# Attention and two feed-forward blocks on one core: phi's row sums, its gate and the last block's scaling placed later, and an addition moved to VectorE

## The chip, the cores and the metric

The kernel runs on one core of a Trainium2 chip. The metric is the device time of one execution in microseconds (us). An execution is compared with others of the same kernel by the median of several runs.

## What is computed

Attention with a linear memory for 4 batches of 8 heads, 576 rows and 64 columns, and behind it two feed-forward blocks:

```python
scores = scale * np.matmul(q, k.transpose(0, 1, 3, 2))
scores = np.where(causal, -1000000000.0, scores)
scores = scores - scores.max(-1, keepdims=True)
a = np.exp(scores)
a /= a.sum(-1, keepdims=True) + 1e-09
local = np.matmul(a, v)
q_p = phi(q)                       # phi(x) = where(x > 0, x, exp(x) - 1) + 1
mem_ret = np.einsum('bhsd,bhde->bhse', q_p, M_prev)
mem_norm = np.einsum('bhsd,bhd->bhs', q_p, z_prev)[..., None] + 1e-06
mem_out = mem_ret / mem_norm
g = 1.0 / (1.0 + np.exp(-beta))[None, :, None, None]
out = g * mem_out + (1 - g) * local
# x: (2304, 512), the heads side by side
h = x @ w_in;  x = (h * np.tanh(softplus(h))) @ w_out      # 512 -> 2048 -> 512
out = (((x @ w1) * (x @ w2)) @ w3) @ w_out2                # 512 -> 1024 -> 512
```

## The kernel before, in words

The attention stage runs over 16 pairs of heads, `p` = 0 to 15, and one turn of the loop (L563) is called a period here. In a period the scores of pair `p` are made while the values of pair `p - 1` are multiplied and those of pair `p + 1` are prepared. The 576 rows of a head are cut into four blocks of 128 rows, numbered 0 to 3, and a last block that holds the remaining 64 rows of both heads.

For a block, `s_blocks` (L397) and `s_last` (L413) let TensorE write scores to a PSUM tile `psA`. VectorE adds the mask and takes the maxima (`maxed`, L389 and L390, a custom instruction and a read of its accumulator). ScalarE makes the exponentials and their sums (`expd`, L395). `normed` (L370) turns the sums to reciprocals (L376, L377) and scales the rows (L381): block by block on VectorE, and on GpSimd for the four numbers in `ON_POOL`. The scaled rows are transposed by TensorE and copied by ScalarE (`pt_g`, L438, copies at L447), and `pv` (L449) multiplies them by the values. The result is rounded by ScalarE (L468) and its remainder taken by VectorE (L79) into `xt`.

In a period the blocks come in the order 3, 2, then 0 and 1 together, then the last. `prep` makes transposed q and k of the next pair in between.

The memory part is `prep_phi` (L332). ScalarE takes the exponential of q (L340), GpSimd makes q + 1 (L341), VectorE joins both to phi (L342). GpSimd multiplies phi by z (L344, the tile `qz`), VectorE sums the rows (L351, the tile `dn`), GpSimd adds 1e-6 (L352), VectorE takes the reciprocal (L353) and multiplies by the gate (L354), and GpSimd multiplies phi by that (L357). `trans_phi` (L362) transposes the result one period later. `qz` and the tile of q + 1 share one buffer.

From pair 4 to pair 11 each period also decodes one piece of the first feed-forward weights, which lie in memory as 64-bit numbers: six VectorE steps (L110 to L121) and three GpSimd steps (L125, L76, L79). `drip` (L546) gives out a few of these steps at a time between the blocks. The tile `da` has one buffer, so the first step of a piece, L110, waits for the last GpSimd step of the piece before.

The order of the instructions comes from a scheduler, which keeps to the order edges written in the program: `tc.issue_after(i)` puts what stands in the block behind instruction `i` on `i`'s engine. `split_x[0]` is the last remainder that `pv` took, `taken[0]` the last maxima. Before, the row sums of phi and the last block's scaling carry the edge behind `split_x[0]`:

```python
            if split_x[0] is not None:
                k_.enter_context(tc.issue_after(split_x[0]))
            nc.vector.tensor_reduce(out=dn, in_=qz, axis=mybir.AxisListType.X, op=ALU.add)
        nc.gpsimd.tensor_scalar(out=dn, in0=dn, scalar1=1e-6, scalar2=1.0, op0=ALU.add, op1=ALU.mult)
```

Behind the attention stage come the two feed-forward blocks, which hold TensorE busy for most of the time.

Of the kernel before, what the change touches and what calls it, by code (L numbers as in the profile page):

```python
# [14 lines left out]
ALU = mybir.AluOpType  # L15
# [6 lines left out]
def fused_kernel(ctx: ExitStack, tc, q, k, v, M_prev, z_prev, beta, w_in, w_out, w1, w2, w3, w_out2, out):  # L22
    nc = tc.nc
    B, H, S, D = q.shape
# [3 lines left out]
    NP = H // 2  # L28
# [300 lines left out]
        st[p]["sum"] = ap_.tile([128, 9], F32, tag="sum", name="sum", bufs=2)  # L329
        st[p]["acc"] = ap_.tile([128, 10], F32, tag="acc", name="acc", bufs=2)  # L330

    def prep_phi(p):  # L332
        b, c = divmod(p, NP)
        qv = st[p]["q"]
        if c == 2 and b + 1 < B:
            load_m(b + 1)
        z = st[p]["z"]
        e = ep.tile([128, NB, 2, D], F32, tag="phie", name="phie", bufs=2)
        u = ep.tile([128, NB, 2, D], F32, tag="ptmp", name="phit", bufs=1)
        nc.scalar.activation(out=e, in_=qv, func=AF.Exp)  # L340
        nc.gpsimd.tensor_scalar(out=u, in0=qv, scalar1=1.0, scalar2=1.0, op0=ALU.add, op1=ALU.mult)  # L341
        nc.vector.scalar_tensor_tensor(out=e, in0=e, scalar=1.0, in1=u, op0=ALU.min, op1=ALU.max)  # L342
        qz = ep.tile([128, NB, 2, D], F32, tag="ptmp", name="qz", bufs=1)
        nc.gpsimd.tensor_tensor(  # L344
            out=qz, in0=e, in1=z[:, None, :, :].to_broadcast([128, NB, 2, D]), op=ALU.mult
        )
        dn = ep.tile([128, NB, 2], F32, tag="dn", name="dn", bufs=2)
        with ExitStack() as k_:
            if split_x[0] is not None:
                k_.enter_context(tc.issue_after(split_x[0]))  # L350
            nc.vector.tensor_reduce(out=dn, in_=qz, axis=mybir.AxisListType.X, op=ALU.add)  # L351
        nc.gpsimd.tensor_scalar(out=dn, in0=dn, scalar1=1e-6, scalar2=1.0, op0=ALU.add, op1=ALU.mult)  # L352
        nc.vector.reciprocal(out=dn, in_=dn)  # L353
        nc.vector.tensor_tensor(  # L354
            out=dn, in0=dn, in1=g_[:, 1:2, 2 * c:2 * c + 2].to_broadcast([128, NB, 2]), op=ALU.mult
        )
        nc.gpsimd.tensor_tensor(  # L357
            out=e, in0=e, in1=dn[:, :, :, None].to_broadcast([128, NB, 2, D]), op=ALU.mult
        )
        st[p]["e"] = e  # L360
# [9 lines left out]
    def normed(p, xs):  # L370

        d = st[p]
        og = ogp[:, p % NP]
        sl = slice(0, 8) if len(xs) > 1 else slice(8, 9)
        rv = d["sum"][:, sl]
        nc.vector.tensor_scalar(out=rv, in0=rv, scalar1=1e-9, scalar2=None, op0=ALU.add)  # L376
        nc.vector.reciprocal(out=rv, in_=rv)  # L377
        for ib, e in xs:
            s = s4[:, 0:S] if ib == 4 else d["s"][ib, e]
            x = 8 if ib == 4 else 2 * ib + e  # L380
            (nc.gpsimd if x in ON_POOL else nc.vector).tensor_scalar(  # L381
                out=s, in0=s, scalar1=d["sum"][:, x:x + 1], scalar2=og[:, x:x + 1], op0=ALU.mult, op1=ALU.mult
            )

    taken = [None]
    split_x = [None]
    copied = [None]

    def maxed(s, o, m, init, a):  # L389
# [59 lines left out]
    def pv(p):  # L449
        b, c = divmod(p, NP)  # L450
        d = st.pop(p)
        V, T, F = d["v"], d["t"], d["phi"]
        pm, pl = psX(), psF()[:, 0:64]
        M_ = mr[b % 2][:, c]
        hv = (UP, DN)
        mm(pm, M_.rearrange("p e d -> p (e d)"), F[:, 0:512], True, False)
        for jb in range(4):
            for e in range(2):
                t, x = T[jb, e, jb]
                mm(pm[hv[e], 128 * jb:512], V[:, jb, e], t[:, x:x + 512 - 128 * jb], False, jb == 3)  # L460
        for e in range(2):
            mm(pl[hv[e]], M_[:, e], F[:, 512:S], True, False)
        for jb in range(5):
            for e in range(2):
                mm(pl[hv[e]], V[:, jb, e], T[4, None, jb][:, hv[e]], False, jb == 4)
        for o, q0, q1 in ((pm, 0, 512), (pl, 512, S)):
            x = xl[b // 2][:, :, c, S * (b % 2) + q0:S * (b % 2) + q1]
            nc.scalar.copy(out=x[:, 0], in_=o[:, 0:q1 - q0])  # L468
            split_x[0] = sub(x[:, 1], o[:, 0:q1 - q0], x[:, 0]).ins

    gt = {}

# [90 lines left out]
    for p in range(NPAIR + 1):  # L563
# [15 lines left out]
        if now:  # L579
            in_turn(s_blocks, p, (3,))  # L580
            if decodes:
                drip(1)
        else:
            in_turn(next, h0)
        if old:
            in_turn(pt_g, p - 1, 1)
# [2 lines left out]
                in_turn(next, h0)  # L589
        if now:  # L590
            in_turn(s_blocks, p, (2,))
            if decodes:
                drip(1)
        if p == 0:
            gate_values(b_)
        if old:
# [25 lines left out]
            normed(p, [(i, e) for e in range(2) for i in range(4)])  # L622
        if p == 0:
            with tc.issue_after(taken[0]):
                prep_phi(0)
        if old:
            in_turn(pv, p - 1)
        if not now:
            split = split_y((0, 0), next(h0))
            early = {(0, 1): emit_h((0, 1))}  # L630
        if now:
            with ExitStack() as k_:
                if old:
                    k_.enter_context(tc.issue_after(split_x[0]))
                normed(p, [(4, None)])
            if decodes:
                drip(7)
        if new:
            with tc.issue_after(taken[0]):
                prep_phi(p + 1)  # L640
        if now and p > 0:
            in_turn(trans_phi, p)
    at.close()
# [248 lines left out]
```

## Time and profile before

| | us |
|---|---|
| median of 3 runs (1028.5 to 1029.44) | 1029.01 |
| the profiled execution | 1029.42 |
| its span, from the first to the last instruction | 1027.6 |

| engine | busy us | share of the span |
|---|---|---|
| TensorE (PE) | 974.8 | 95% |
| TensorE weight load (PEld) | 827.7 | 81% |
| VectorE (DVE) | 617.1 | 60% |
| ScalarE (ACT) | 501.4 | 49% |
| GpSimd (POOL) | 336.8 | 33% |

SP is SyncE, which issues most of the loads. The rows of a timeline give the start of an instruction in us from the start of the span, its length in us, the engine, the line, the operation, what it writes and reads with partitions x elements, and, in brackets, how long the engine had been idle and what ended that. A length can overlap the next instruction's by some 0.1 us, and several instructions of one line in a row are merged (x4).

### The profile page before, as it was taken

Reading aid. Unit: us, or ns where it says so; the run is one execution under the profiler, and the core shown is the slowest. Engines: PE = TensorE matmul, PEld = TensorE weight load, DVE = VectorE, ACT = ScalarE, POOL = GpSimd, SP = SyncE. Lnnn points to the kernel's source line nnn. Section 1 sums busy time; section 2 is a strip of 40 time slices with the busy share of each in tenths; the row PEclk is TensorE's granted clock in tenths of the full one; section 3 lists DMA queues with packets and bytes.
Section 4 is the critical chain, followed back from the end, with each engine's and each line's share of the span. In section 5 each row is a group of like instructions: output and inputs, shape, how many; then the busy total and the mean of one; then the engine's idle time right before and its main releaser. Section 6 shows DMA issues by size and latency. Waiting matters only on the chain.

```text
span 1027.6 us, 15098 instructions
## 1 busy us (share of the span) xinstructions
PE 974.8 (95%) x5584; PEld 827.7 (81%) x5584; DVE 617.1 (60%) x1364; ACT 501.4 (49%) x1016; POOL 336.8 (33%) x345
## 2 busy tenths in 40 slices
PE   6888888889999999999999999999989999999998
PEld 3555555556899999999999999988757888888897
DVE  5678889876366669885988476666973221121111
ACT  5777877776565655655555644442313221221212
POOL 5546686653143344545454212112550000000000
PEclk8999999999999999999999999999999999999999
DMA  7433443310131214232421662222410000100101
GB/s 158 116 70 95 109 109 93 69 30 17 46 123 48 96 62 164 65 112 87 148 103 63 246 228 80 77 78 85 165 48 1 20 22 1 42 1 1 41 1 62
DMA packets 93626, 81.73 MB, mean 80 GB/s; under 512 B 68720, under 2 KB 72816, under 8 KB 93552
## 3 DMA queue, kind: packets, MB, share of 16 engines
q1 hardware_dynamic: 92224, 80.44, 25.3%
q8 instruction: 44, 0.72, 0.3%
q10 hardware_dynamic: 1328, 0.33, 0.2%
q14 instruction: 30, 0.25, 0.1%
HBM read 65.54 MB, written 15.20 MB: 79 GB/s over the span
## 4 chain that ended last, share of the span: by engine, by line
PE 69%; DVE 15%; ACT 6%; DMA 3%; POOL 3%; issue 2%; SPq 1%; POOLq 0%; DVEq 0%; ACTq 0%
PE psA L63 37%; PE psX L63 15%; PE psF L63 14%; DVE s L390 2%; ACT s L395 2%; DVE draw L121 2%; DVE s L381 1%; PE psF L66 1%; ACT pt L447 1%; DVE da L117 1%; DMA draw<-in_moe_w_dram 1%; PE psX L66 1%; DVE phie L342 1%; DVE y L506 1%; DVE draw L120 1%
## 5 line engine op out<-in xcount | busy, mean ns | idle before, releaser
L63 PE MATMUL psA<-xt,wqt 128*128 128x384 f32 x1152 | 208.9, 337 | 2.4 <-DVE y L506 2.2
L125 POOL TENSOR_TENSOR da<-da,draw 128x512 f32<-128x512 f32 x72 | 100.8, 1408 | 326.3 <-DVE draw L121 282.1
L63 PEld LDWEIGHTS psA<-xt,wqt 128*128 128x128 f32 x1152 | 201.5, 189 | 3.9 <-DVE y L506 3.2
L63 PE MATMUL psX<-gh,wqt 128*128 128x384 f32 x480 | 122.3, 335 | 1.1 <-DVE x L673 1.1
L818 DVE TENSOR_TENSOR bs<-bs,psA 128x512 f32<-128x512 f32 (+1 forms) x40 | 25.4, 634 | 160.0 <-ACT bs L817 160.0
L63 PE MATMUL psA<-x2h,w12t 128*128 128x512 f32 (+1 forms) x384 | 107.1, 357 | 6.8 <-DVE bs L818 4.6
L817 ACT COPY bs<-psA 128x512 f32<-128x512 f32 (+1 forms) x40 | 21.8, 544 | 160.6 <-PE psA L63 150.6
L395 ACT ACTIVATE s<-s,acc 128x512 f32<-128x512 f32 (+2 forms) x144 | 85.5, 600 | 28.9 <-DVE acc L390 28.5
L66 PEld LDWEIGHTS psF<-ident,s 128*128 128x128 f32 x400 | 44.9, 145 | 55.8 <-ACT pt L447 26.8
L63 PE MATMUL psA<-x2s,w12t 128*128 128x512 f32 x384 | 89.7, 389 | 0.0
L66 PE MATMUL psF<-ident,s 128*128 128x128 f32 x400 | 66.4, 292 | 23.8 <-ACT pt L447 14.9
L63 PEld LDWEIGHTS psX<-gh,wqt 128*128 128x128 f32 x480 | 86.9, 188 | 2.2 <-DVE x L673 1.4
L493 ACT ACTIVATE y<-psA 128x384 f32<-128x384 f32 x96 | 41.9, 490 | 90.2 <-PE psA L63 90.1
L63 PEld LDWEIGHTS psA<-x2h,w12t 128*128 128x128 f32 x384 | 68.3, 189 | 20.8 <-DVE bs L818 5.0
L63 PEld LDWEIGHTS psA<-x2s,w12t 128*128 128x128 f32 x384 | 72.1, 188 | 14.9
L390 DVE CUSTOM_DVE_ANT_0 s<-psA,mask 128x512 f32<-128x512 f32 (+2 forms) x144 | 62.8, 480 | 31.0 <-PE psA L63 30.8
L506 DVE TENSOR_TENSOR y<-y,psA 128x384 f32<-128x384 f32 x96 | 48.6, 549 | 53.4 <-ACT y L504 53.4
L63 PE MATMUL psX<-gl,wqt 128*128 128x384 f32 x240 | 80.4, 336 | 0.0
L63 PE MATMUL psF<-gh,wqt 128*128 128x384 f32 x288 | 73.1, 334 | 0.0
L63 PE MATMUL psA<-room,w12t 128*128 128x512 f32 (+1 forms) x192 | 68.0, 354 | 0.0
L447 ACT COPY pt<-psF 128x512 f32<-128x512 f32 (+1 forms) x112 | 58.9, 540 | 17.7 <-PE psF L66 17.6
L63 PE MATMUL psX<-wft,room 128*128 128x512 f32 x216 | 61.6, 391 | 0.3 <-DVE wft L79 0.3
(117 smaller groups left out, 1871.7 us busy)
## 6 DMA issues: line engine op xcount, KB each, us to landing
draw<-in_moe_w_dram SPq DMA_DIRECT2D x32, 512.0 KB, 3.7
draw<-in_moe_w_out_dram SPq DMA_DIRECT2D x24, 512.0 KB, 3.5
draw<-in_moe_w_in_dram SPq DMA_DIRECT2D x16, 512.0 KB, 4.5
out_dram<-ob SPq DMA_DIRECT2D x18, 256.0 KB, 2.0
raw<-in_q_dram SPq DMA_DIRECT2D x32, 128.0 KB, 2.8
raw<-in_v_dram SPq DMA_DIRECT2D x32, 128.0 KB, 3.0
o_dram<-draw SPq DMA_DIRECT2D x8, 512.0 KB, 2.8
w_dram<-draw SPq DMA_DIRECT2D x8, 512.0 KB, 2.8
```

The source lines that it names most:

```text
L63: tail[0] = nc.tensor.matmul(o, lhsT=l, rhs=r, start=start, stop=stop).ins
L66: tail[0] = nc.tensor.transpose(o, src, ident).ins
L117: lambda: V.scalar_tensor_tensor(out=ai, in0=hw, scalar=-0x40000000, in1=ai, op0=ALU.bitwise_and, op1=ALU.bitwise_or),
L121: lambda: V.scalar_tensor_tensor(out=lw.bitcast(F32), in0=lw.bitcast(U32), scalar=2.0 ** -52, in1=hw.bitcast(F32), op0=ALU.mult, op1=ALU.mult,
L125: lambda: nc.gpsimd.tensor_tensor(out=a, in0=a, in1=lw.bitcast(F32), op=ALU.add),
L390: taken[0] = nc.vector.tensor_tensor_reduce(out=s, in0=o, in1=m, op0=ALU.add, op1=ALU.min, scale=-scale, scalar=init, accum_out=a,).ins
L395: nc.scalar.activation(out=s, in_=s, func=AF.Exp, scale=-1.0, bias=a, accum_out=r)
L447: copied[0] = nc.scalar.copy(out=t[:, 0:n], in_=o[:, 0:n]).ins
L493: nc.scalar.activation(out=y[m // 2][:, m % 2], in_=hp[m], func=AF.Tanh, scale=0.5)
L506: nc.vector.tensor_tensor(out=y[i][:, j], in0=y[i][:, j], in1=hp[2 * i + j], op=ALU.mult)
L817: nc.scalar.copy(out=bs, in_=pb)
L818: nc.vector.tensor_tensor(out=bs, in0=bs, in1=pa, op=ALU.mult)
```

## The change

`prep_phi` is cut in two. `phi_terms` makes phi and the product with z, and the product now stands behind GpSimd's scaling of the pair before (`scaled[0]`, set in `normed`). `phi_norm` makes the row sums, adds 1e-6 on VectorE, takes the reciprocal and multiplies by the gate. `phi_norm` of pair `p` and the last block's `normed` of pair `p - 1` move from the end of a period into the next one, behind the maxima of block 2, with an edge behind the last maxima taken. In the title of the change the blocks are counted from one, and block 2 is the third. One call of `drip` goes, so that the rest of the piece takes one step more.

```diff
-    def prep_phi(p):
+    def phi_terms(p):
...
-        nc.gpsimd.tensor_tensor(
-            out=qz, in0=e, in1=z[:, None, :, :].to_broadcast([128, NB, 2, D]), op=ALU.mult
-        )
+        with tc.issue_after(scaled[0]):
+            nc.gpsimd.tensor_tensor(
+                out=qz, in0=e, in1=z[:, None, :, :].to_broadcast([128, NB, 2, D]), op=ALU.mult
+            )
+        st[p]["e"] = e, qz
+
+    def phi_norm(p):
+        c = p % NP
+        e, qz = st[p]["e"]
         dn = ep.tile([128, NB, 2], F32, tag="dn", name="dn", bufs=2)
-        with ExitStack() as k_:
-            if split_x[0] is not None:
-                k_.enter_context(tc.issue_after(split_x[0]))
-            nc.vector.tensor_reduce(out=dn, in_=qz, axis=mybir.AxisListType.X, op=ALU.add)
-        nc.gpsimd.tensor_scalar(out=dn, in0=dn, scalar1=1e-6, scalar2=1.0, op0=ALU.add, op1=ALU.mult)
+        nc.vector.tensor_reduce(out=dn, in_=qz, axis=mybir.AxisListType.X, op=ALU.add)
+        nc.vector.tensor_scalar(out=dn, in0=dn, scalar1=1e-6, scalar2=None, op0=ALU.add)
         nc.vector.reciprocal(out=dn, in_=dn)
...
-            (nc.gpsimd if x in ON_POOL else nc.vector).tensor_scalar(
+            r = (nc.gpsimd if x in ON_POOL else nc.vector).tensor_scalar(
                 out=s, in0=s, scalar1=d["sum"][:, x:x + 1], scalar2=og[:, x:x + 1], op0=ALU.mult, op1=ALU.mult
             )
+            if x in ON_POOL:
+                scaled[0] = r.ins
...
         else:
+            normed(p - 1, [(4, None)])
             in_turn(next, h0)
...
             in_turn(s_blocks, p, (2,))
-            if decodes:
-                drip(1)
+            if old:
+                with tc.issue_after(taken[0]):
+                    normed(p - 1, [(4, None)])
+                    phi_norm(p)
...
         if p == 0:
             with tc.issue_after(taken[0]):
-                prep_phi(0)
+                phi_terms(0)
+                phi_norm(0)
...
-        if now:
-            with ExitStack() as k_:
-                if old:
-                    k_.enter_context(tc.issue_after(split_x[0]))
-                normed(p, [(4, None)])
-            if decodes:
-                drip(7)
         if new:
             with tc.issue_after(taken[0]):
-                prep_phi(p + 1)
+                phi_terms(p + 1)
+        if decodes:
+            drip(7)
```

The lines behind L332 move by a few numbers: the maxima are at L395, the scalings at L384, the row sums at L354, the addition at L355, reciprocal and gate at L356 and L357, the product with z at L345 and phi's last product at L360.

On VectorE, in a period that decodes, between the remainders of one pair and the first two blocks' maxima of the next, this order stood before (s_113 is the last block, s_1711 and s_1736 are blocks 3 and 2 of the first head, s_1783 is block 0, dn holds phi's row sums; of each block's maxima the first instruction is shown):

```order
L79 TENSOR_TENSOR xt_81<-psF,xt_81 128x64
L376 TENSOR_SCALAR sum<-sum 128x1
L351 TENSOR_REDUCE dn<-qz 128x10
L377 RECIPROCAL sum<-sum 128x1
L390 ISA s_1711,acc<-psA,mask 128x512
L381 TENSOR_SCALAR s_113<-s_113,sum,ogp 128x576
L353 RECIPROCAL dn<-dn 128x10
L354 TENSOR_TENSOR dn<-dn,gates 128x10
L390 ISA s_1736,acc<-psA,mask 128x384
L110 TENSOR_SCALAR da<-draw 128x512
L390 ISA s_1783,acc<-psA,mask 128x128
```

And this order stands there now (s_1702 and s_1727 are blocks 3 and 2, s_1782 is block 0):

```order
L79 TENSOR_TENSOR xt_81<-psF,xt_81 128x64
L395 ISA s_1702,acc<-psA,mask 128x512
L395 ISA s_1727,acc<-psA,mask 128x384
L379 TENSOR_SCALAR sum<-sum 128x1
L354 TENSOR_REDUCE dn<-qz 128x10
L380 RECIPROCAL sum<-sum 128x1
L110 TENSOR_SCALAR da<-draw 128x512
L355 TENSOR_SCALAR dn<-dn 128x10
L384 TENSOR_SCALAR s_113<-s_113,sum,ogp 128x576
L356 RECIPROCAL dn<-dn 128x10
L357 TENSOR_TENSOR dn<-dn,gates 128x10
L395 ISA s_1782,acc<-psA,mask 128x128
```

The sums, the gate and the last block's scaling have moved behind the maxima of blocks 3 and 2, and the addition has joined them.

On GpSimd, in the same period, from the product with z to q for the last block of the next pair (`qd`), this stood before (phit is q + 1, phie is phi, wqt the decoded weights):

```order
L344 TENSOR_TENSOR qz<-phie,zr 128x640
L381 TENSOR_SCALAR s_1783<-s_1783,sum,ogp 128x128
L381 TENSOR_SCALAR s_1711<-s_1711,sum,ogp 128x512
L125 TENSOR_TENSOR da<-da,draw 128x512
L352 TENSOR_SCALAR dn<-dn 128x10
L341 TENSOR_SCALAR phit<-raw 128x640
L76 TENSOR_SCALAR wqt<-da 128x512
L357 TENSOR_TENSOR phie<-phie,dn 128x640
L79 TENSOR_TENSOR wqt<-da,wqt 128x512
L324 TENSOR_TENSOR qd<-qt,own 128x128
```

And this stands there now (of the four scalings the first two are shown in both):

```order
L384 TENSOR_SCALAR s_1782<-s_1782,sum,ogp 128x128
L384 TENSOR_SCALAR s_1702<-s_1702,sum,ogp 128x512
L345 TENSOR_TENSOR qz<-phie,zr 128x640
L125 TENSOR_TENSOR da<-da,draw 128x512
L76 TENSOR_SCALAR wqt<-da 128x512
L79 TENSOR_TENSOR wqt<-da,wqt 128x512
L341 TENSOR_SCALAR phit<-raw 128x640
L360 TENSOR_TENSOR phie<-phie,dn 128x640
L324 TENSOR_TENSOR qd<-qt,own 128x128
```

The scalings have passed the product with z, the decoded piece has passed phi's two steps, and the addition is gone. TensorE's order is the same in both; on ScalarE one exponential of block 1 and a copy have changed places.

## Rows read from the trace of the kernel before

**Rows 1.** Busy time by stretch; columns PE, PEld, DVE, ACT, POOL, clock, DMA share, GB/s
```profile
0.00:250.00 250.00, 211.60 (x1520) 129.42 (x1520) 190.92 (x600) 184.01 (x529) 149.70 (x181) 0.98 0.37 87
250.00:1027.60 777.60, 763.17 (x4066) 698.27 (x4064) 426.23 (x765) 317.36 (x488) 187.11 (x164) 1.00 0.22 77
```
**Rows 2.** Timeline of VectorE in a plain period, pair 12 to pair 13
```profile
204.03 0.46 DVE L390 CUSTOM_DVE_ANT_0 s<-psA,mask 128x288 f32<-128x288 f32 x1 [1.86 <-PE psA L63]
...
206.15 2.45 DVE L381 TENSOR_SCALAR s<-s,sum,ogp 128x256 f32<-128x256 f32 x4
208.52 0.68 DVE L79 TENSOR_TENSOR xt<-psX,xt 128x512 fp32r<-128x512 f32 x1
...
210.22 0.58 DVE L381 TENSOR_SCALAR s<-s,sum,ogp 128x576 f32<-128x576 f32 x1
...
211.15 0.54 DVE L354 TENSOR_TENSOR dn<-dn,gates 128x10 f32<-128x10 f32 x1
211.61 0.68 DVE L390 CUSTOM_DVE_ANT_0 s<-psA,mask 128x512 f32<-128x512 f32 x1
...
219.23 0.46 DVE L390 CUSTOM_DVE_ANT_0 s<-psA,mask 128x288 f32<-128x288 f32 x1 [1.62 <-PE psA L63]
```
**Rows 3.** Timeline of GpSimd in the same period
```profile
205.87 1.54 POOL L344 TENSOR_TENSOR qz<-phie,zr 128x640 f32<-128x640 f32 x1 [3.46 <-DVE sum L376]
207.40 2.95 POOL L381 TENSOR_SCALAR s<-s,sum,ogp 128x128 f32<-128x128 f32 x4
210.44 0.42 POOL L352 TENSOR_SCALAR dn<-dn 128x10 f32<-128x10 f32 x1
```
**Rows 4.** Timelines of TensorE and ScalarE in the same period
```profile
208.48 1.13 PE L63 MATMUL psA<-kt,qt 64*128 64x512 f32 x4
...
210.29 0.58 ACT L447 COPY pt<-psF 128x512 f32<-128x512 f32 x1 [0.64 <-PE psF L66]
212.33 0.72 ACT L395 ACTIVATE s<-s,acc 128x512 f32<-128x512 f32 x1 [1.46 <-DVE acc L390]
```
**Rows 5.** Timeline of VectorE in a decode period, pair 8 to pair 9
```profile
140.86 0.46 DVE L390 CUSTOM_DVE_ANT_0 s<-psA,mask 128x288 f32<-128x288 f32 x1
...
143.55 0.20 DVE L377 RECIPROCAL sum<-sum 128x8 f32<-128x8 f32 x1
143.67 1.92 DVE L121 SCALAR_TENSOR_TENSOR draw<-draw 128x512 f32<-128x512 uint32 x1
...
148.75 0.67 DVE L390 CUSTOM_DVE_ANT_0 s<-psA,mask 128x512 f32<-128x512 f32 x1
...
149.96 1.13 DVE L381 TENSOR_SCALAR s<-s,sum,ogp 128x576 f32<-128x576 f32 x1
...
151.50 0.55 DVE L390 CUSTOM_DVE_ANT_0 s<-psA,mask 128x384 f32<-128x384 f32 x1
...
154.25 0.43 DVE L110 TENSOR_SCALAR da<-draw 128x512 int32<-128x512 int32 x1 [1.72 <-POOL wqt L79]
...
156.62 0.46 DVE L390 CUSTOM_DVE_ANT_0 s<-psA,mask 128x288 f32<-128x288 f32 x1
```
**Rows 6.** Timeline of GpSimd in the same period
```profile
145.03 3.38 POOL L381 TENSOR_SCALAR s<-s,sum,ogp 128x128 f32<-128x128 f32 x4
148.38 1.28 POOL L125 TENSOR_TENSOR da<-da,draw 128x512 f32<-128x512 f32 x1
...
150.74 0.82 POOL L76 TENSOR_SCALAR wqt<-da 128x512 fp32r<-128x512 f32 x1
...
152.94 1.27 POOL L79 TENSOR_TENSOR wqt<-da,wqt 128x512 fp32r<-128x512 f32 x1
```
**Rows 7.** Timelines of VectorE and GpSimd at pair 15, where no product with z is made
```profile
251.25 1.45 DVE L381 TENSOR_SCALAR s<-s,sum,ogp 128x256 f32<-128x256 f32 x4
...
251.42 3.04 POOL L381 TENSOR_SCALAR s<-s,sum,ogp 128x128 f32<-128x128 f32 x4 [8.23 <-DVE sum L377]
```
**Rows 8.** All instructions of line 121: shortest, median, longest in ns
```profile
L121 DVE SCALAR_TENSOR_TENSOR draw<-draw x72: 676/687/1922, 80.8 to 764.1; 128x512 f32<-128x512 uint32 x72
```

More of the change, by code (lines that the diff above doesn't have):

```diff
@@ L380, in normed @@
             x = 8 if ib == 4 else 2 * ib + e
-            (nc.gpsimd if x in ON_POOL else nc.vector).tensor_scalar(
+            r = (nc.gpsimd if x in ON_POOL else nc.vector).tensor_scalar(
                 out=s, in0=s, scalar1=d["sum"][:, x:x + 1], scalar2=og[:, x:x + 1], op0=ALU.mult, op1=ALU.mult
             )
+            if x in ON_POOL:
+                scaled[0] = r.ins
     taken = [None]
-    split_x = [None]
+    scaled = [None]
     copied = [None]
@@ L468, in pv @@
             nc.scalar.copy(out=x[:, 0], in_=o[:, 0:q1 - q0])
-            split_x[0] = sub(x[:, 1], o[:, 0:q1 - q0], x[:, 0]).ins
+            sub(x[:, 1], o[:, 0:q1 - q0], x[:, 0])
     gt = {}
```

## The prediction

> **What bounds the kernel now.** I first split the span where the attention stage ends. In the first 250 us TensorE is busy for 211.6 us, in the rest for 763.2 of 777.6 [rows 1]. Nothing that the diff touches runs in the second part, so it counts with its length unchanged, and what the change saves or costs before it moves the end one for one.
>
> Then I read the periods of the attention stage, engine by engine, on the timelines. There are 16, one for each pair of heads; I count a period from the maxima of the last block of rows (L390 on 128x288, "last maxima" below) to the next such maxima, and write +x for x us after them. Two kinds occur. A **plain period** decodes no weights: 204.03 to 219.23, 15.20 us. A **decode period** carries one weight piece along: 140.86 to 156.62, 15.76 us.
>
> In the plain period VectorE reaches the third block's maxima (128x512) at 211.61, which is +7.58 [rows 2]. They need TensorE's scores, done at 209.61 [rows 4], 2.0 us earlier. What holds them up stands in front of them in VectorE's queue: the gate multiplication at 211.15 waits for GpSimd's addition of 1e-6, at 210.44, and that stands in GpSimd's queue behind the product with z (1.54 us) and four scalings (2.95 us) [rows 3]. ScalarE, idle 1.46 us for these maxima, starts its exponentials at 212.33 [rows 4]. From there to the next last maxima it is 6.90 us of ScalarE work, two transposes and the last block's matmuls.
>
> In the decode period the third block's maxima start at 148.75, +7.89, behind VectorE's unbroken work; then VectorE waits 1.72 us for GpSimd's last subtraction of the decoded piece before it may start the next piece (L110) [rows 5, 6].
>
> **The change, part by part.** (1) The 1e-6. Sixteen GpSimd instructions go, of up to 0.42 us each [rows 3]; sixteen VectorE additions of the same ten columns come. No row shows one; the nearest is the multiplication of the same ten columns, 0.54 us at the longest [rows 2], and below nothing it cannot cost. I take 0.1 us a period, since the instruction has one input instead of two, and keep both ends. The wait for GpSimd disappears from VectorE's queue.
>
> (2) Row sums, gate and the scaling of the last block go behind the maxima of blocks three and two of the next period (the order rows show that the second block's maxima are passed too). Behind them stand the first two blocks' maxima. What reads the moved results comes late enough: the last block's transposes at the end of the period, those of phi in the next one.
>
> (3) On GpSimd the four scalings now stand ahead of the product with z, and the decoded piece ahead of phi's two steps. TensorE's transposes wait for the scalings, so they gain.
>
> (4) On SyncE's queue the load of z moves behind those of v; its consumer runs a period later, so I book nothing. Two ScalarE copies change places with an exponential; nothing either.
>
> **Plain period, worked out.** Ahead of the third block's maxima remain phi (L342), the sums, four scalings and the two splits of the output. In the row of before the splits end at about +5.3 even with scalings of 2.45 us [rows 2]. So the maxima can start when TensorE is done, at +5.6. Next in line is ScalarE's copy of the first transposes, 210.29 with 0.58: it starts at +6.26, its successor can start at about +6.74 [rows 4]. The exponentials start there in place of +8.30; with the 6.90 us behind them the period is 13.64, a gain of 1.56. I take **1.5 us**. The gain cannot be above 2.0 (TensorE's scores); low end 1.0, if half a microsecond of new waiting arises before the first two blocks.
>
> Which intervals count: between the last maxima of pairs 2 and 3, 3 and 4, 11 and 12, 12 and 13, 13 and 14, 14 and 15, that is six. Pairs 3 and 11 border on decoding, but no L110 waits there for a piece before it. 6 x 1.5 = 9.0.
>
> **Decode period, worked out.** On VectorE the sums' reciprocal ends at about +2.9 now (143.55 plus latency [rows 5]); of what stands ahead of it, one decode step of some 0.4 us is exchanged for another, so it stays at 2.9. GpSimd's scalings, now first, start at +3.0 in place of +4.17 (145.03) [rows 6]. They take 3.04 [rows 7] to 3.38, the product 1.54 [rows 3], then the piece: 1.28, 0.82, 1.27 and some 0.2 between them [rows 6]. The subtraction ends at about 3.0 + 3.2 + 1.5 + 3.4 + 0.2 = +11.3, where before it ended at 154.21, +13.35.
>
> From L110 to the next last maxima it was 156.62 - 154.25 = 2.37 us [rows 5]. One decode step of some 0.45 (like L110's row) leaves this stretch; the last block's scaling with reciprocal and gate, 149.96 to 151.50, 1.54 us, and the addition enter it: 3.5 us. So 11.3 + 3.5 = 14.8 against 15.76, a gain of **0.95 us**. There are seven such intervals (pairs 4 to 11): 6.7.
>
> The other chain of this period is not longer. Ahead of the third block's maxima stand, from +2.9: 0.33, the scalings 1.45 [rows 7], the long decode step L121, the splits, some 0.7 [rows 2]. L121 lasts 1.92 us here and 0.69 in the median of all 72 [rows 5, 8]: here it overlaps GpSimd's two-input product, which leaves that place. So they start at +6.1 to +7.3; with 0.72 to the exponentials and 6.90 the period would be 13.7 to 14.9.
>
> Ends for the decode period: 13.65, if nothing on GpSimd gets in the way (gain 2.1), and 15.3, if every GpSimd step is the longest of its rows and VectorE's scaling meets phi's first step (the 1.13 for 576 columns [rows 5] against 0.58 for the same form in the plain period's row [rows 2]).
>
> The first two intervals are ruled by loads and by GpSimd's first queue; between nothing and two plain gains I take 1.2 together.
>
> **Sum.** 9.0 + 6.7 + 1.2 = 16.9. The profiled execution took 1029.4 (span 1027.6 and 1.8 around it), 0.4 above the median of the runs, 1029.0; 1029.4 - 16.9 = **1012.5 us**.
>
> **Rivals.** *A, slower.* The two groups of scalings now begin at the same moment, VectorE's at +2.1 (plain) or +3.2 (decode) and GpSimd's beside them. If VectorE had to wait for GpSimd's group, 3.04 us would be added ahead of the third block's maxima: plain 2.1 + 3.04 + 1.45 + 0.72 = 7.3, period 14.9, gain 0.3; decode 3.2 + 3.04 + 1.45 + 0.6 + 0.72 = 9.0, and 9.0 + 0.72 + 6.90 = 16.6, a loss of 0.9. Sum 6 x 0.3 - 7 x 0.9 = -4.5, or 1034. It decides from about 2 us of waiting on: 6.1 + 2.0 + 0.72 + 6.90 is the 15.7 of before. For it: VectorE's scalings take 2.45 beside GpSimd's product and 1.45 alone; L121 stretches alike. Against it: at pair 15 both groups already start together, at 251.25 and 251.42, and take 1.45 and 3.04 [rows 7], end to end 3.2 us, less than the sum of 4.5. I give it 5%. The Trainium skill ("SBUF — State Buffer", who interferes with whom) has it that a VectorE instruction in a two-port mode and any GpSimd instruction hold one port pair exclusively, and that the second is blocked in full; that would be rival A. The rows with the product agree, the rows of pair 15 do not.
>
> *B, decode hardly gains.* If L121 keeps its length beside GpSimd's scalings and phi's step delays VectorE's last decode step as well, the period is some 15.3, gain 0.45: 9.0 + 3.2 + 0 = 12, or 1017. For it: GpSimd's steps carry L110 in both versions. 20%.
>
> *C, decode at its other chain.* Period 13.7 to 13.9, gain 2 in seven intervals: 9.4 + 14 + 1.2 = 24.6, or 1005. The first period's half clock might add to it: the stage's mean granted clock is 0.98 [rows 1]. 15%.
>
> *D, no change:* the z load or the raw loads come late in the shorter periods and give the gain back. Against it: each is issued about a period ahead. 3%.
>
> **How the numbers follow.** Forecast 57%, B 20, C 15, A 5, D 3. The forecast's own spread is 1008 to 1016; with B above and C below the range is **1004 to 1020**, which leaves out the rest of C's low side, A and D. Faster by over 0.2% (2 us, about what a measurement of this kernel can tell from none) holds for the forecast, B and C: 0.92; within it D, 0.03; slower A, 0.05.
>
> **What would show it.** In the profile after, plain periods should be 13.6 to 14.2 long, with the third block's maxima waiting for TensorE and the gate multiplication nowhere ahead of them. Decode periods should be 14.4 to 15.2, with L110 still waiting for GpSimd's subtraction, at about +11.3, and L121 near 0.7. VectorE's four scalings should last about 1.45 beside GpSimd's. The part behind the attention stage should keep its 777 us. I am wrong if the scalings of VectorE come near 4 us, if the first two blocks' maxima wait for the product with z, or if the gain is lost behind 250 us.

## The result and the profile after

The changed kernel takes 1014.45 us (median of 4 runs, 1013.33 to 1015.73); the kernel before, beside it, 1029.22 (1028.5 to 1029.45). The ratio is 0.9858, with a 95% interval of 0.9841 to 0.9875. The forecast was 1012.5 with a range of 1004 to 1020: right in direction and nearly in size. The profiled execution took 1015.02 us, 14.40 less than that of before; its span is 1013.2.

Busy time by stretch (the stage now ends at 235; columns as in [rows 1]):

```profile
0.00:235.00 235.00, 210.21 (x1520) 129.07 (x1520) 179.57 (x617) 183.41 (x530) 144.54 (x165) 0.98 0.40 93
235.00:1013.20 778.20, 763.17 (x4066) 697.80 (x4064) 425.94 (x765) 317.35 (x488) 187.29 (x164) 1.00 0.23 77
```

Behind the stage TensorE is busy for the same 763.17 us as in [rows 1]. What went is idle time of TensorE in the stage: 250 - 211.6 = 38.4 us before, 235 - 210.2 = 24.8 now.

**A plain period after**, pair 12 to pair 13: VectorE, GpSimd and ScalarE in the timeline, to set beside [rows 2 to 4]:

```profile
194.54 0.46 DVE L395 CUSTOM_DVE_ANT_0 s<-psA,mask 128x288 f32<-128x288 f32 x1 [0.93 <-PE psA L63]
...
196.66 1.45 DVE L384 TENSOR_SCALAR s<-s,sum,ogp 128x256 f32<-128x256 f32 x4
...
200.17 0.69 DVE L395 CUSTOM_DVE_ANT_0 s<-psA,mask 128x512 f32<-128x512 f32 x1 [1.01 <-PE psA L63]
...
208.19 0.46 DVE L395 CUSTOM_DVE_ANT_0 s<-psA,mask 128x288 f32<-128x288 f32 x1 [1.62 <-PE psA L63]
...
196.81 3.07 POOL L384 TENSOR_SCALAR s<-s,sum,ogp 128x128 f32<-128x128 f32 x4 [2.00 <-DVE sum L380]
...
199.84 1.55 POOL L345 TENSOR_TENSOR qz<-phie,zr 128x640 f32<-128x640 f32 x1
...
200.80 0.59 ACT L452 COPY pt<-psF 128x512 f32<-128x512 f32 x1 [0.64 <-PE psF L66]
201.28 0.72 ACT L400 ACTIVATE s<-s,acc 128x512 f32<-128x512 f32 x1
```

The period is 208.19 - 194.54 = 13.65 us instead of 15.20. The third block's maxima (200.17, +5.63) now wait 1.01 us for TensorE's scores instead of standing behind the sums, the scaling and the gate. ScalarE's copy starts at +6.26, and the exponential follows it without idle time at +6.74, where before it sat idle 1.46 us for VectorE [rows 4]. VectorE's scalings take 1.45 us beside GpSimd's 3.07; the product with z no longer overlaps them.

**A decode period after**, pair 9 to pair 10, VectorE and GpSimd, to set beside [rows 5, 6]:

```profile
150.97 0.44 DVE L395 CUSTOM_DVE_ANT_0 s<-psA,mask 128x288 f32<-128x288 f32 x1
...
154.11 1.74 DVE L384 TENSOR_SCALAR s<-s,sum,ogp 128x256 f32<-128x256 f32 x4
155.78 0.68 DVE L121 SCALAR_TENSOR_TENSOR draw<-draw 128x512 f32<-128x512 uint32 x1
...
157.10 0.68 DVE L395 CUSTOM_DVE_ANT_0 s<-psA,mask 128x512 f32<-128x512 f32 x1
...
162.44 0.94 DVE L110 TENSOR_SCALAR da<-draw 128x512 int32<-128x512 int32 x1 [1.75 <-POOL wqt L79]
...
165.88 0.44 DVE L395 CUSTOM_DVE_ANT_0 s<-psA,mask 128x288 f32<-128x288 f32 x1
...
154.03 3.53 POOL L384 TENSOR_SCALAR s<-s,sum,ogp 128x128 f32<-128x128 f32 x4 [2.66 <-DVE sum L380]
157.53 1.54 POOL L345 TENSOR_TENSOR qz<-phie,zr 128x640 f32<-128x640 f32 x1
...
161.13 1.27 POOL L79 TENSOR_TENSOR wqt<-da,wqt 128x512 fp32r<-128x512 f32 x1
162.37 0.73 POOL L341 TENSOR_SCALAR phit<-raw 128x640 f32<-128x640 f32 x1
```

The period is 14.91 us instead of 15.76. L110 still waits for GpSimd's subtraction, as long as before (1.75 us against 1.72), but the whole chain starts earlier: GpSimd's scalings at +3.06 instead of +4.17. L121 is back at 0.68 us. L110 itself has grown from 0.43 to 0.94 us, and GpSimd starts L341 just as it begins; in e7, where L341 starts later, it keeps to 0.43. The last block's scaling takes 0.57 us there, where it took 1.13 before [rows 5].

**The first full period**, where the change loses. VectorE, GpSimd and TensorE, and the stretches behind (columns as in [rows 1]):

```profile
22.83 0.82 DVE L354 TENSOR_REDUCE dn<-qz 128x10 f32<-128x640 f32 x1 [2.08 <-POOL qz L345]
...
25.24 0.55 DVE L395 CUSTOM_DVE_ANT_0 s<-psA,mask 128x384 f32<-128x384 f32 x1
...
18.22 3.07 POOL L384 TENSOR_SCALAR s<-s,sum,ogp 128x128 f32<-128x128 f32 x4 [3.81 <-ACT s L400]
21.25 1.54 POOL L345 TENSOR_TENSOR qz<-phie,zr 128x640 f32<-128x640 f32 x1
...
32.29 0.55 PE L66 MATMUL psF<-ident,phie 128*128 128x128 f32 x3 [2.23 <-ACT pt L452]
32.67 1.63 PE L63 MATMUL psA<-kt,qd 128*128 128x288 f32 x4
```

```profile
32.00:34.00 2.00, 1.71 (x7) 1.43 (x8) 1.00 (x4) 2.00 (x7) 0.48 (x1) 0.79 0.25 53
34.00:38.00 4.00, 4.00 (x13) 1.20 (x13) 2.47 (x8) 0.99 (x3) 4.00 (x5) 0.68 0.36 82
```

phi of pair 0 has no earlier period in which its product could be made. VectorE waits 2.08 us for that product, now behind GpSimd's scalings, and the second block's maxima queue behind. Later TensorE is idle for 2.23 us, and behind that its granted clock is 0.79 and 0.68 of full speed in the mean of the two stretches; between 34 and 36 us it is 0.50, the lower of its two levels (1.2 and 2.4 GHz). Before it was 1.00 in both stretches, behind an idle time of 1.90 us in the same place:

```profile
31.55 0.55 PE L66 MATMUL psF<-ident,phie 128*128 128x128 f32 x3 [1.90 <-ACT pt L447]
```

The last maxima of pair 2 come at 49.14 us instead of 47.60.

Where the 14.40 us came from, interval by interval between last maxima (a minus is a loss):

| intervals | forecast | measured |
|---|---|---|
| up to pair 2 | +1.2 | -1.5 |
| six plain (2 to 4, 11 to 15) | +9.0 | +10.7 |
| seven decode (4 to 11) | +6.7 | +5.9 |
| behind pair 15's last maxima | 0 | -0.7 |
| sum | 16.9 | 14.4 |

### The profile page after: what moved, and what is told of

Its sections match the earlier page's. It is cut to its first block, busy times and chain, and to the rows that moved or that the text cites. A ratio compares the mean times of both kernels' runs of the same rounds, so it can differ in the third digit from the quotient of the medians.

```text
span 1013.2 us, 15098 instructions
## 1 busy us (share of the span) xinstructions
PE 973.4 (96%) x5584; PEld 826.9 (82%) x5584; DVE 605.5 (60%) x1380; ACT 500.8 (49%) x1016; POOL 331.8 (33%) x329
## 3 DMA queue, kind: packets, MB, share of 16 engines
HBM read 65.54 MB, written 15.20 MB: 80 GB/s over the span
## 4 chain that ended last, share of the span: by engine, by line
PE 71%; DVE 12%; POOL 7%; ACT 6%; issue 2%; DMA 2%; POOLq 0%; SPq 0%; DVEq 0%; ACTq 0%
PE psA L63 37%; PE psX L63 17%; PE psF L63 14%; ACT s L400 2%; POOL s L384 2%; DVE s L395 2%; POOL da L125 2%; PE psF L66 1%; DMA draw<-in_moe_w_dram 1%; DVE da L117 1%; DVE da L110 1%; POOL qz L345 1%; ACT pt L452 1%; DVE da L111 1%; DVE da L114 1%
## 5 line engine op out<-in xcount | busy, mean ns | idle before, releaser
L395 DVE CUSTOM_DVE_ANT_0 s<-psA,mask 128x512 f32<-128x512 f32 (+2 forms) x144 | 63.4, 482 | 25.8 <-PE psA L63 25.5
L66 PE MATMUL psF<-ident,s 128*128 128x128 f32 x400 | 62.9, 289 | 10.8 <-DVE s L384 6.2
L384 POOL TENSOR_SCALAR s<-s,sum,ogp 128x128 f32<-128x128 f32 (+1 forms) x64 | 53.6, 849 | 46.3 <-DVE sum L380 30.5
```

Source lines behind the costliest of these rows:

```text
L66: tail[0] = nc.tensor.transpose(o, src, ident).ins
L384: r = (nc.gpsimd if x in ON_POOL else nc.vector).tensor_scalar(out=s, in0=s, scalar1=d["sum"][:, x:x + 1], scalar2=og[:, x:x + 1], op0=ALU ...
L395: taken[0] = nc.vector.tensor_tensor_reduce(out=s, in0=o, in1=m, op0=ALU.add, op1=ALU.min, scale=-scale, scalar=init, accum_out=a,).ins
```

## The experiments

The runs were made in three batches (e1 to e4, e5 to e8, e9 to e11), each beside the kernel before, which took 1031.76, 1032.79 and 1033.02 us there; ratios are to that, and times of different batches are best set side by side through them. The medians are of all runs, the other columns of the one profiled execution. "Behind" is the span less the start of pair 15's last maxima. All times are in us.

| run | median | ratio, 95% interval | pair 1 at | pair 1 to 2 | plain | decode | pair 15 at | behind |
|---|---|---|---|---|---|---|---|---|
| before | 1029.22 | | 34.01 | 13.59 | 15.2 | 15.75 | 249.68 | 777.9 |
| the change | 1014.45 | 0.9858, 0.9841 to 0.9875 | 34.74 | 14.40 | 13.65 | 14.90 | 234.61 | 778.6 |
| e1 | 1014.36 | 0.9831, 0.9811 to 0.9852 | 33.80 | 12.74 | 13.65 | 14.9 | 231.93 | 779.7 |
| e2 | 1016.12 | 0.9841, 0.9824 to 0.9859 | 34.58 | 12.75 | 13.65 | 15.00 | 234.63 | 779.5 |
| e3 | 1008.74 | 0.9779, 0.9761 to 0.9797 | 34.62 | 14.39 | 13.65 | 14.07 to 14.13 | 228.74 | 778.3 |
| e4 | 1023.35 | 0.9917, 0.9897 to 0.9937 | 34.97 | 14.26 | 13.65 | 15.47 to 16.84 | 244.24 | 779.6 |
| e5 | 1028.16 | 0.9960, 0.9944 to 0.9976 | 34.52 | 14.26 | 15.00 | 15.46 | 247.49 | 781.1 |
| e6 | 1030.28 | 0.9980, 0.9966 to 0.9995 | 33.92 | 13.78 | 15.22 | 15.77 | 249.42 | 781.0 |
| e7 | 1013.35 | 0.9821, 0.9793 to 0.9849 | 35.60 | 12.75 | 13.65 | 14.58 | 231.53 | 778.8 |
| e8 | 1008.76 | 0.9772, 0.9749 to 0.9795 | 34.05 | 12.75 | 13.64 | 14.06 | 226.50 | 781.6 |
| e9 | 1028.82 | 0.9975, 0.9959 to 0.9992 | 34.16 | 13.61 | 15.21 | 15.52 | 249.93 | 778.4 |
| e10 | 1015.61 | 0.9847, 0.9824 to 0.9870 | 34.80 | 14.40 | 13.65 | 14.90 | 234.58 | 781.2 |
| e11 | 1012.01 | 0.9807, 0.9782 to 0.9832 | 34.17 | 14.40 | 13.65 | 14.58 | 231.84 | 778.4 |

"Plain" is the common value; some of the six intervals differ. From pair 11 to 12 it is 15.75 before and 13.76 in the change, but 15.00 in e2 and 15.49 in e4. From 2 to 3 e6 and e9 take 16.0, where before takes 15.21, and TensorE's clock falls to 0.50 there; e9 takes 16.0 from 13 to 14, too. The last one, 14 to 15, is 15.22 before, 13.92 in e6 and 12.77 in the change.

### e1: the first product set free

```diff
-        with tc.issue_after(scaled[0]):
+        with ExitStack() as k_:
+            if p > 0:
+                k_.enter_context(tc.issue_after(scaled[0]))
```

> The change, but for pair 0 alone the product with z stands ahead of GpSimd's scalings again. Theory (first interval): VectorE waited 2.08 us for this product in period 1, which held up the second block's maxima, left TensorE idle until 32.3 us and so cost a spell at the lower of its two clocks in pair 0's value products. Then the product ends near 19.5 us instead of 22.8, the last maxima of pair 1 come at 33.5 to 34.0 us (34.74 with the change), those of pair 2 at 46.3 to 47.6 (49.14), the mean clock between 32 and 38 us is back at 1.0, and the time falls by 1.5 to 2.8 us to about 1012.3. Rival (the loads or ScalarE rule this interval): both stay within 0.3 us of the change's, the time too.

Measured: the starts as expected, pair 1 at 33.80 and pair 2 at 46.54. VectorE and TensorE in the same period (the row sums' line is L356 in this kernel):

```profile
20.52 0.81 DVE L356 TENSOR_REDUCE dn<-qz 128x10 f32<-128x640 f32 x1
...
31.34 0.55 PE L66 MATMUL psF<-ident,phie 128*128 128x128 f32 x3 [1.66 <-ACT pt L454]
31.72 1.14 PE L63 MATMUL psA<-kt,qd 128*128 128x288 f32 x4
```

The 2.08 us wait is gone, the sums come 2.3 us earlier, and the four matmuls take 1.14 us instead of 1.63 at a clock of 1.00. The stage ends 2.7 us earlier than in the change, 0.9 of it by pair 1 and 1.65 in the next interval. The time, 1014.36, is not the 1012.3 expected. By the ratio it is 0.27% below the change (0.9831 against 0.9858), but the two intervals overlap, so the times don't settle it.

### e2: no product held behind the scalings

```diff
-        with tc.issue_after(scaled[0]):
-            nc.gpsimd.tensor_tensor(
+        nc.gpsimd.tensor_tensor(
```

> The change without the edge that puts the product with z behind the scalings, in all periods: GpSimd's product stands first again. Theory (the decode period is carried by GpSimd's steps up to L110, the plain one by TensorE's scores and ScalarE): plain periods stay at 13.65 us. In decode periods GpSimd can start the product before the sums' reciprocal is there, so its last subtraction ends some 0.8 us earlier, but VectorE's scalings and L121 meet the product again (2.45 instead of 1.74, or 1.9 instead of 0.68), the third block's maxima start at about +7.1 instead of +6.1, and the period is 14.1 to 14.8 us (14.90 with the change); pair 1 comes as early as in the run with the product of pair 0 ahead. Time 1009 to 1012.5. Rival (the gain of the decode period comes from taking the product away from beside L121): decode periods go back to 15.4 or more, time 1016 or more.

Measured: plain 13.65, decode 15.00, just outside what either side expected; the time, 1016.12, is 3.6 us above the theory's range and where the rival had it. Pair 1 comes at 34.58, not as early as in e1. In the plain periods the sums have a period's time, so it hardly matters where the product stands. In the decode period VectorE's timeline shows the price:

```profile
152.40 1.66 DVE L120 TENSOR_SCALAR draw<-da 128x512 int32<-128x512 int32 x1
...
160.77 0.94 DVE L110 TENSOR_SCALAR da<-draw 128x512 int32<-128x512 int32 x1 [0.28 <-POOL wqt L79]
```

L120, 0.43 us in e7's trace where the product comes later, takes 1.66 beside it here and delays what VectorE does behind it. The wait for the subtraction shrinks to 0.28 us, and the chain of the third block's maxima (+7.38, with 0.72 and 6.90 behind it 15.0) carries the period.

### e3: two buffers for the decoded piece

```diff
-    decoder(at, 2, 1)
+    decoder(at, 2, 2)
```

> The change with two buffers instead of one for the decoder's tile da in the attention stage, so that L110 no longer waits for GpSimd's subtraction. Theory (L110's wait of 1.75 us carries the decode period): the wait goes, the decode period falls from 14.90 to between 13.65 (the plain period's chain) and 14.2, seven times, so 5 to 8.7 us: time 1006 to 1009.5. Rival (ScalarE's chain or VectorE's load carries it and the wait at L110 is idle time that costs nothing): decode periods stay at 14.7 to 14.9, time within 1.5 us of the change.

Measured: decode 14.07 to 14.13, as expected, and 5.9 us less in the stage. So L110's wait did carry the decode period after the change. In VectorE's timeline L110 no longer waits, though it still meets the product:

```profile
154.15 1.01 DVE L110 TENSOR_SCALAR da<-draw 128x512 int32<-128x512 int32 x1
```

### e4: the last block's scaling left in its old place

Row sums, addition, gate and product stand as in the change.

```diff
+        if now:
+            with ExitStack() as k_:
+                if old:
+                    k_.enter_context(tc.issue_after(split_x[0]))
+                normed(p, [(4, None)])
...
-                    normed(p - 1, [(4, None)])
                     phi_norm(p)
```

> The change with the last block's scaling left where it was, ahead of the third block's maxima; row sums, addition and gate are moved as in the change. Theory: in the plain period the scaling (0.6 us with its reciprocal) fits between the splits and ScalarE's copy of the first transposes, so 13.65 stays, give or take 0.2. In the decode period the stretch from L110 to the last maxima gets 0.5 us shorter, so 14.3 to 14.5: time 1010.5 to 1013. Rival (moving the scaling is a part of the gain): plain periods 14.2 or more, time 1017 or more.

Measured: plain as expected (13.65), decode a miss: 15.47, and three periods of 16.6 to 16.8. VectorE and GpSimd in one of the long ones, and its end by stretch:

```profile
162.90 1.91 DVE L384 TENSOR_SCALAR s<-s,sum,ogp 128x576 f32<-128x576 f32 x1
164.72 0.68 DVE L396 CUSTOM_DVE_ANT_0 s<-psA,mask 128x512 f32<-128x512 f32 x1
...
173.22 0.46 DVE L396 CUSTOM_DVE_ANT_0 s<-psA,mask 128x288 f32<-128x288 f32 x1 [1.98 <-PE psA L63]
...
162.94 1.54 POOL L345 TENSOR_TENSOR qz<-phie,zr 128x640 f32<-128x640 f32 x1
```

```profile
166.00:170.00 4.00, 2.20 (x15) 1.39 (x16) 3.57 (x16) 4.00 (x13) 2.90 (x4) 0.90 0.51 150
170.00:173.00 3.00, 3.00 (x12) 2.62 (x12) 1.23 (x5) 3.00 (x13) 1.54 (x2) 0.57 0.82 184
```

In its old place the scaling meets the product: 1.91 us, where it takes 0.57 alone. The third block's maxima slip to +8.34. In the long periods TensorE, busy for 2.20 of 4 us, then runs at 0.57 of its clock. So the plain periods owe nothing to the scaling's move, and the decode periods over half a microsecond each. The interval from pair 11 to 12, 15.49 here, goes with the decode periods.

### e5: the last block's scaling alone moved

```diff
+            if old:
+                with tc.issue_after(taken[0]):
+                    normed(p - 1, [(4, None)])
...
-                normed(p, [(4, None)])
```

> The kernel before, with the last block's scaling alone moved behind the third block's maxima of the next period; row sums, the addition on GpSimd and the gate stay where they were. Theory (the plain period is held by the gate, which waits for GpSimd's addition behind the product and the scalings): the scaling's 0.58 us lay beside that wait, so a plain period stays at 15.0 to 15.25 us; in a decode period the scaling already stood behind the third block's maxima, so it stays at 15.5 to 15.9. The time is 3 us below to 2 us above the kernel before, ratio 0.997 to 1.002. Rival (VectorE's own work ahead of the third block's maxima is what holds them, and each 0.58 us counts): plain periods 14.5 to 14.7, 4 us or more below.

Measured: plain 15.00, decode 15.46, 4.6 us below before: the theory's kind, but 1.6 us more than it allowed, and the decode periods just below its 15.5. The rival's periods of 14.5 to 14.7 fall, though the time is as far below as it asked (4 us or more). VectorE, pair 13 to pair 14:

```profile
219.51 2.45 DVE L381 TENSOR_SCALAR s<-s,sum,ogp 128x256 f32<-128x256 f32 x4
...
224.06 0.22 DVE L353 RECIPROCAL dn<-dn 128x10 f32<-128x10 f32 x1 [0.64 <-POOL dn L352]
```

Without the scaling VectorE simply waits there, 0.64 us, for GpSimd's addition.

### e6: the addition alone moved to VectorE

```diff
-        nc.gpsimd.tensor_scalar(out=dn, in0=dn, scalar1=1e-6, scalar2=1.0, op0=ALU.add, op1=ALU.mult)
+        nc.vector.tensor_scalar(out=dn, in0=dn, scalar1=1e-6, scalar2=None, op0=ALU.add)
```

> The kernel before, with the 1e-6 alone added by VectorE. Theory: in a plain period the sums still wait behind the product, the splits and the scaling in VectorE's queue, and the gate starts at most 0.3 us earlier: 14.9 to 15.25 us. In a decode period up to 0.4 us leaves GpSimd's queue ahead of the subtraction that L110 waits for: 15.35 to 15.8. Together 0 to 4 us below the kernel before, ratio 0.996 to 1.000. Rival (the wait for GpSimd's addition alone is what held the plain period): plain 14.4 to 14.7 and 5 us or more below.

Measured: plain 15.22 and decode 15.77, at the upper ends of the theory's ranges and no shorter than before. The 2.5 us in the medians do not show in these periods; one interval is longer (2 to 3) and one shorter (14 to 15) than before. VectorE and GpSimd, pair 12 to pair 13:

```profile
211.34 1.07 DVE L381 TENSOR_SCALAR s<-s,sum,ogp 128x576 f32<-128x576 f32 x1
...
212.65 0.68 DVE L390 CUSTOM_DVE_ANT_0 s<-psA,mask 128x512 f32<-128x512 f32 x1
...
211.38 0.72 POOL L341 TENSOR_SCALAR phit<-raw 128x640 f32<-128x640 f32 x1
```

The wait is gone, but GpSimd, free of the addition, starts L341 earlier, and VectorE's scaling takes 1.07 us beside it instead of 0.58. The maxima start at +7.59, as before (+7.58).

### e7: the change with the addition left on GpSimd

The edit is that of e6 reversed, made to the change.

> The whole change, but with the 1e-6 still added by GpSimd. Theory: once the sums and the gate stand behind the maxima of blocks 3 and 2, the engine of the addition matters little. Plain periods stay at 13.6 to 13.7, since the gate is no longer ahead of anything that TensorE or ScalarE wait for; in decode periods the addition stands behind the subtraction in GpSimd's queue, so that the gate comes some 0.3 to 0.8 us later: 14.9 to 15.4. The time is 0 to 4 us above the changed kernel. Rival (the wait for GpSimd was the cost, wherever it stands): plain 14.2 or more, 6 us or more above.

Measured: plain 13.65, as expected; decode 14.58, better than the change's 14.90, where 14.9 to 15.4 was expected. VectorE and GpSimd, pair 9 to pair 10:

```profile
159.99 0.43 DVE L110 TENSOR_SCALAR da<-draw 128x512 int32<-128x512 int32 x1 [1.73 <-POOL wqt L79]
160.34 0.57 DVE L384 TENSOR_SCALAR s<-s,sum,ogp 128x576 f32<-128x576 f32 x1
...
160.05 0.44 POOL L355 TENSOR_SCALAR dn<-dn 128x10 f32<-128x10 f32 x1
160.57 0.93 POOL L341 TENSOR_SCALAR phit<-raw 128x640 f32<-128x640 f32 x1
```

The small addition now stands between the subtraction and L341. L110 meets it and stays at 0.43 us, where in the change it meets L341 and takes 0.94. Moving the 1e-6 to VectorE thus cost some 0.3 us in each decode period and brought nothing in the plain ones.

The first periods go another way than in the change. Pair 1 comes at 35.60, 0.9 us later, and the next interval is 12.75. TensorE's longest idle time lies earlier here, and so does the fall of its clock:

```profile
27.26 1.11 PE L66 MATMUL psF<-ident,s 128*128 128x128 f32 x4 [3.45 <-ACT pt L452]
```

```profile
28.00:30.00 2.00, 2.00 (x11) 1.05 (x10) 1.64 (x4) 1.37 (x4) 0.79 (x3) 0.50 0.89 215
```

### e8: two buffers, and the first product set free

The edits of e1 and e3 together.

> The change with two buffers for the decoded piece, and with the product with z of pair 0 not held behind GpSimd's scalings. If the two costs are separate, the gains add up: the first two intervals as with the product alone (last maxima of pairs 1 and 2 at 33.8 and 46.5 us), decode periods as with two buffers (14.07 to 14.13), the attention stage ends 2.2 to 2.7 us earlier than with two buffers alone, pair 15's last maxima at 226.0 to 226.5, and the time is 1.5 to 3.5 us below that run, ratio 0.973 to 0.977 to the kernel before. Rival (the stage behind, or its loads, give the first period's gain back): the span shrinks by less than 1 us though pair 15 comes 2 us earlier.

Measured: pair 15 at 226.50, 2.24 us ahead of e3, so in the stage the two gains nearly add up. But the time is that of e3, as the rival had it: in the profiled execution, the slowest of its four, 781.6 us go by behind the stage instead of 778.3. By stretch:

```profile
718.00:722.00 4.00, 1.72 (x5) 1.13 (x6) 4.00 (x7) 2.13 (x4) 1.34 (x1) 0.86 0.47 157
722.00:726.00 4.00, 4.00 (x14) 3.13 (x14) 4.00 (x6) 0.08 (x1) 3.12 (x3) 0.71 0.51 165
...
752.00:756.00 4.00, 4.00 (x13) 3.16 (x12) 1.64 (x3) 1.20 (x2) 0.00 (x0) 0.62 0.00 0
```

In the second feed-forward block TensorE waits for VectorE (1.72 us busy in 4), and its clock then falls to 0.71, later to 0.62; in e3 it is 1.00 between 700 and 764 us. Whether this comes with the edit or with the execution is open.

### e9: two buffers in the kernel before

The edit of e3, made to the kernel before.

> The kernel before with two buffers for the decoded piece. Theory (before, a decode period had two chains of nearly equal length, L110 behind GpSimd, and the third block's maxima behind VectorE's work at +7.89): with the first chain gone the second holds, 149.46 for the exponential plus 6.90 is +15.5, so a decode period is 15.2 to 15.6 us instead of 15.75, and the kernel 1 to 4 us below before, ratio 0.996 to 0.999; on the changed kernel the same edit gave 0.8 us a period. Rival (the buffer alone was what held the decode periods): 14.9 to 15.0 or less, 5 us or more below before.

Measured: decode 15.52, as expected: 0.23 us a period, where the same edit gives the change 0.8. The time is 4.2 us below before. In the profiled execution two plain intervals of 16.0, with the clock down to 0.50 and 0.57, take the stage's gain back (pair 15 at 249.93). VectorE at the end of such a period:

```profile
156.59 0.46 DVE L390 CUSTOM_DVE_ANT_0 s<-psA,mask 128x288 f32<-128x288 f32 x1 [1.22 <-PE psA L63]
```

With L110 out of the way VectorE waits 1.22 us for TensorE: the other chain, that of the third block's maxima, holds the period.

### e10: the change once more

> The changed kernel once more, on this chip, to stand beside the two runs of this batch and the one with the addition on GpSimd: last maxima of pairs 1, 2, 15 at 34.7, 49.1 and 234.6 us, decode periods 14.90, the clock below full between 32 and 38 us; ratio 0.984 to 0.988. Rival (the half clock of the first period comes at random, whatever the order): full clock there and pair 2 at 47.4.

Measured: the same starts within 0.1 us, and the same fall of the clock (0.76 and 0.69 in the two stretches). So in this order of work it came in both executions that were profiled. Behind the stage, though, this execution takes 781.2 us where the first took 778.6.

### e11: the addition on GpSimd, and the first product set free

The edits of e7 and e1 together.

> The change with the 1e-6 still added by GpSimd and the product with z of pair 0 not held behind GpSimd's scalings. If both costs are real and separate: decode periods 14.56 to 14.60 as with the addition on GpSimd, pair 1's last maxima at 33.8 to 34.6 and pair 2's 12.75 later, pair 15's at 229.2 to 230.2, and 1 to 5 us below the changed kernel of this batch. Rival (the 0.33 us a decode period that the addition on GpSimd gave came from the shifted first period): decode periods 14.9.

Measured: decode 14.58 again, so that gain does not come from the first period. Pair 1 comes at 34.17, but the next interval is 14.40 after all, not 12.75. TensorE:

```profile
31.71 0.55 PE L66 MATMUL psF<-ident,phie 128*128 128x128 f32 x3 [2.02 <-ACT pt L454]
32.10 1.59 PE L63 MATMUL psA<-kt,qd 128*128 128x288 f32 x4
```

The clock falls here (0.66 and 0.50 from 32 to 36 us) without the wait for the first product. So pair 15 comes at 231.84, where 229.2 to 230.2 was expected. The time is 3.6 us below that of the change in the same batch (1012.01 against 1015.61, with no overlap of their runs).

## Why the prediction was nearly right, and where it failed

**Plain periods: right, but the reason given was half of it.** 13.65 against a worked-out 13.64; copy and exponential start at +6.26 and +6.74, as worked out. The prediction laid the delay of before to the gate's wait for GpSimd's addition. But VectorE is idle there for only 0.1 us:

```profile
209.31 0.80 DVE L351 TENSOR_REDUCE dn<-qz 128x10 f32<-128x640 f32 x1
...
210.90 0.22 DVE L353 RECIPROCAL dn<-dn 128x10 f32<-128x10 f32 x1
```

The scaling ahead of the reciprocal ends at 210.80, and the addition it waits for at 210.86 [rows 2, 3]. So two chains came out nearly level: GpSimd's queue, and VectorE's own work from the sums to the gate, 2.3 us up to the maxima at 211.61. The change takes both out of the way. e5 and e6, which each shorten one of the two, gain 0.2 us and nothing. I booked 1.5 us of the 1.56, and two of the six gained more: 1.99 between pairs 11 and 12, where I had taken a plain period for one of before that took 15.75, and 2.45 between 14 and 15, above the 2.0 that I had called the most. TensorE's clock had been at 0.50 between 245 and 247 us there and is now 1.00; in e6, where it was 1.00 too, this interval took 13.92. Of the parts, the sums and the gate behind the maxima are left to carry the gain: e4 has it without the scaling's move, e2 without the product's, e7 without the addition's. No run moves the sums and the gate alone.

**Decode periods: right in mechanism, 0.1 us a period short.** L110 starts behind the subtraction at +11.47 (forecast +11.3), and from there it is 3.44 us (forecast 3.5). e3 shows that this wait is the bound. What was too short is GpSimd's chain, its scalings above all (3.53 where I took 3.2). That the 3.5 came out is partly luck: L110 took 0.94 where I took 0.43, and the scaling 0.57 where I took the 1.13 of before.

**The first two intervals, "between nothing and two plain gains I take 1.2 together": this is the term that failed.** It measured -1.5. I had listed as a sign of error that the first two blocks' maxima wait for the product with z, but worked the order out for a steady period only. In the first one the second block's maxima do wait, and the first two blocks' behind them: the step "On GpSimd the four scalings now stand ahead of the product with z", booked there at nothing, costs VectorE 2.08 us there. e1 takes that back, 0.9 us by pair 1, and comes to pair 2 at 46.54, 1.06 us ahead of the kernel before and near the 1.2 booked. The other 1.65 us come with the fall of the clock behind TensorE's idle stretch: the interval is 14.40 with it (the change, e3, e10, e11; 14.26 in e4) and 12.75 without (e1, e2, e8). In e7 the fall comes earlier, behind the 3.45 us, and is paid before pair 1. It is not bound to the product's place: e5, the kernel before with the scaling moved, has it too (14.26). At this place the clock fell in the six traces in which TensorE had been idle for 2.02 to 2.23 us (the change, e3, e4, e5, e10, e11) and stayed at 1.00 in the seven with 1.43 to 1.90. What decides it the runs do not show.

**Behind the stage: 0 booked, 0.7 lost**, and open. It takes 777.9 us in the trace of before and between 778.3 and 781.6 in the twelve others, and two executions of the same kernel, the change and e10, differ by 2.6. So nothing of this size there can be laid to the change.

**The rivals.** A (VectorE's scalings wait for GpSimd's) did not happen; they took 1.45 us beside GpSimd's 3.07, 1.74 beside 3.53. The rule that spoke for it, in the Trainium skill ("SBUF — State Buffer", who interferes with whom), has a second instruction at the shared port pair blocked in full. That fits the product's rows (L120 at 1.66, the scaling at 1.91 in e4) but not scalings beside scalings. B asked for L121 to keep its 1.92 us; it fell to 0.68. C, decode periods at the other chain, would have needed the second buffer: with it they are 14.07. D did not happen.

**The parts in the sum.** That 1e-6 costs "0.1 us a period" on VectorE was right for the instruction (0.15 us) and wrong for the kernel: e7 shows 0.3 us a decode period lost to what GpSimd does in the freed slot.

The lowest ratios are those of the change with two buffers (e3 at 0.9779, e8 at 0.9772). Setting the first product free is worth 2.2 to 2.7 us in the stage, and whether it shows in the time stays open. Two buffers with the addition left on GpSimd were not run together.

## What to carry to other kernels

Where an engine's queue holds a result that is wanted only later, ahead of one that others wait for now, move the first behind the second. Here each run that kept this move kept the gain of the plain periods, and the scaling or the addition alone brought little. Cost such a move in the first turn of the loop too, where nothing of an earlier turn covers it. When a period has two chains of nearly equal length, a fix to one pays only what the other leaves (0.23 us a period in e9, 0.8 in e3).

## What was unexpected of the hardware

- An instruction taken off GpSimd can slow VectorE: GpSimd's next one starts earlier and overlaps another VectorE instruction. L110 went from 0.43 to 0.94 us beside L341, the scaling of 576 columns from 0.58 to 1.07 in e6.
- Beside GpSimd's product with two inputs an integer step and a scaling of VectorE stretch by over a microsecond (0.43 to 1.66 in e2, 0.57 to 1.91 in e4). Not everything does: the third block's maxima, read from PSUM, keep to 0.69 beside it (200.17 beside 199.84 in the change), and beside GpSimd's scalings four VectorE scalings keep to 1.45 or 1.74 us.
- Behind an idle time of TensorE of 2.02 to 2.23 us inside the stage the granted clock fell to 0.50, and the 12.75 us of an interval became 14.40; behind 1.43 to 1.90 us in the same place it stayed at 1.00. A small shift of the work moves such a fall, or makes it: e7 has it earlier, e6 and e9 have one between pairs 2 and 3 that the kernel before doesn't.
